# A table of 1,574 entries orders all operations of a fused attention and gated-MLP kernel, in place of its list scheduler

## The chip, the core and the metric

The kernel runs on one core of a Trainium2 chip. The core has four engines that work on data: TensorE (PE in the profile; its weight loads are a row of their own, PEld), VectorE (DVE), ScalarE (ACT) and GpSimd (POOL). SyncE (SP) issues nearly all transfers. Each engine takes its instructions in the order in which the program issues them; an instruction that waits for another engine or for a transfer holds up all that stands behind it on its own engine. The metric is the device time of one execution, in microseconds.

## What is computed

The reference, cut to what matters: capped attention over 4 batches of 12 heads, 448 positions and 64 columns, and behind it a gated MLP with a spatial gate.

```python
scores = scale * np.matmul(q, k.transpose(0, 1, 3, 2))
scores = cap * np.tanh(scores / cap)
attn = np.exp(scores - max); attn = attn / (np.sum(attn, -1) + 1e-09)
x = np.matmul(attn, v)                       # heads side by side: (4, 448, 768)
h = gelu_tanh(x @ w_in)                      # 1024 columns
u, v = h[..., :512], h[..., 512:]
v_n = (v - mean) / np.sqrt(var + 1e-06) * g_ln
v_s = np.einsum('ts,bsd->btd', w_sg, v_n) + b_sg[None, :, None]
out = x + (u * v_s) @ w_out
```

## The kernel before

**Tiling.** The 12 heads of a batch are six pairs; a pair is called batch.pair here, so 0.3 is the fourth pair of batch 0. Two pairs make a group. The 448 key positions of a pair are three blocks of 128 and a tail of 64; the tails of both pairs of a group are worked on together, as block 0 of the first pair. A unit is one block: `scores` (matmuls into one of two PSUM tiles `sc`), tanh and exp on ACT over 128x896 (L635, L637) into one of five tiles `p`, and `values` (L594, L604). There are 84 units. Most scores and the MLP's matmuls run as three products of a high and a low part, so that q and k, the weights and the activations are split first: a cast gives the high part (`cop`, L338 on DVE or L340 on ACT), a subtraction on DVE the low part (`sub`, L368). q and k of a pair lie in one of three tiles `raw`.

**Sums.** The softmax denominators are matmuls with ones (`den_op`, L504). In nine of twelve groups DVE first adds the `p` tiles of a pair (`add`, L647). `recip` copies the sums out, sends them through DRAM (four transfers out, one in), takes reciprocals on DVE (L683, L686) and sends them out again four times; `norm` reads each pair's row back, spread over 128 partitions (L725, tile `n`), and multiplies (L728).

**MLP of a batch (`gated`).** `hv` (L785), `hu` (L825), `vsg` (L842) and `outp` (L863) are the matmul groups; `hv 0.3` is tile 0, chunk 3. Between them lie gelu (L766 and L771 on ACT, L768 and L773 on DVE), layer norm and the gate. They accumulate in PSUM tiles `ps`, of which there are three.

**Weights.** w_in and w_out come as 64-bit words and are decoded: `decode` loads a piece of 512 or 384 KB into one of six stages (L420), four operations on DVE or ACT take the words apart (L426, L432, L436, L441), one on POOL adds them (L446), and a cast and a subtraction split the result.

**What sets the order.** All this is recorded as operations by `op`, each with its engine (or two engines, `BOTH`, for casts and copies), an estimated cost, a key and its buffers. `Plan.run` (L173) is a list scheduler: it steps an estimated clock, takes from the operations that are ready on an engine the one with the least key, chooses the engine of a `BOTH` operation, and issues it. The order in which it issues is the program order of each engine. The keys come from numbers at the top of the file (`ATT`, `GATED`, `FETCH_W` and others).

**Transfers.** `fetch` (L536) loads q and k of a pair in two transfers of 224 KB, from arrays `q2` and `k2`. Only the very first, q of pair 0.0, is issued on ACT's queue; SP issues the rest.

Of the kernel before, what the change touches and what calls it, by code (L numbers as in the profile page):

```python
# [49 lines left out]
DEN = 14.19  # L50
TVAL = 21.27
TPOS = 1
TPOS0 = 3
DEC_AHEAD = 219.05

ISSUE = 0.45
LAT = {
    ("pe", "pe"): 0.0, ("pe", "pool"): 0.08, ("pe", "act"): 0.04, ("pe", "dve"): 0.04, ("pe", "sp"): 0.03,
    ("act", "act"): 0.025, ("act", "dve"): 0.033, ("act", "pe"): 0.052, ("act", "pool"): 0.08, ("act", "sp"): 0.03,
    ("dve", "dve"): 0.031, ("dve", "act"): 0.034, ("dve", "pe"): 0.054, ("dve", "pool"): 0.08, ("dve", "sp"): 0.03,  # L60
    ("pool", "pool"): 0.03, ("pool", "act"): 0.035, ("pool", "dve"): 0.035, ("pool", "pe"): 0.054,
    ("pool", "sp"): 0.03, ("sp", "sp"): 0.03, ("sp", "pe"): 0.06, ("sp", "act"): 0.04, ("sp", "dve"): 0.04,
    ("sp", "pool"): 0.08,
}
OVERLAP = {"act": 0.099, "dve": 0.08, "pool": 0.0, "sp": 0.0, "pe": 0.0}
# [18 lines left out]
class Buf:  # L84
    def __init__(self, pool=None, t=None, cls=None):
        self.pool, self.t, self.cls = pool, t, cls
        self.hist, self.left, self.end = [], 0, 0.0
        self.queued = pool is None
        self.on_free = None
        self.first = None  # L90


class Pool:
    def __init__(self, tiles, caps=None):
        self.free = [(-1.0, i, t) for i, t in enumerate(tiles)]
        self.n = len(tiles)
        self.queues = {}
        self.caps = caps or {}
        self.held = {}

    def add(self, when, t):
        self.free.append((when, self.n, t))
        self.n += 1

    def can(self, bufs):
        by = {}
        for b in bufs:
            k = by.get(b.cls, 0)
            q = self.queues[b.cls]
            if len(q) <= k or q[k] is not b:  # L110
                return None
            by[b.cls] = k + 1
            if self.held.get(b.cls, 0) + k + 1 > self.caps.get(b.cls, 99):
                return None
        if len(self.free) < len(bufs):
            return None
        return sorted(self.free)[len(bufs) - 1][0]

    def take(self, b):
        e = min(self.free)  # L120
        self.free.remove(e)
        self.queues[b.cls].popleft()
        self.held[b.cls] = self.held.get(b.cls, 0) + 1
        b.t = e[2]
# [12 lines left out]
class Plan:
# [3 lines left out]
    def op(self, eng, cost, fn, rd=(), wr=(), key=0.0, mode=None, size=0, fast=False):  # L141
        o = Op()
        o.engs = {eng: (cost, fn)} if isinstance(eng, str) else {e: (cost(e), lambda e=e: fn(e)) for e in eng}
        o.key, o.mode, o.size, o.fast = round(key, 6), mode, size, fast
        o.succ, o.weak, o.npred, o.ready, o.alloc, o.num = [], [], 0, 0.0, [], len(self.ops)
# [27 lines left out]
    def run(self):  # L173
        engines = ("pe", "act", "dve", "pool", "sp")
        free = dict.fromkeys(engines, 0.0)
        cand = {e: [] for e in engines}
        mode, wire, left, last = None, 0.0, len(self.ops), 0.0
        port = {"dve": 0.0, "pool": 0.0}

        def ready(o):  # L180
            for e in o.engs:
                cand[e].append(o)

        for o in self.ops:
            if not o.npred:
                ready(o)
        while left:
            best = None
            for e in engines:
                ests, f = [], free[e]  # L190
                for o in cand[e]:
                    t = o.ready if o.ready > f else f
# [778 lines left out]
```

## Time and profile before

| what | us |
|---|---|
| median of 3 runs | 383.86 (381.99 to 384.19) |
| the profiled execution: span from first to last instruction | 380.5 |
| the same execution, outside its span | not shown; the median lies 3.4 above the span |
| PE busy in the span | 371.8 |
| DVE busy | 297.5 |
| ACT busy | 229.4 |
| POOL busy | 43.2 |

The granted TensorE clock is 1.00 in every slice of the span but the last, after the matmuls. Rows of the trace have the start in us from the span's start, the duration, the engine, the line, the operation and the tiles (output <- inputs). Matmul records overlap, since matmuls are pipelined and their ends are modelled. Where PE works without a pause is therefore read from the distance between starts, not from the busy share.

### The profile page before, as it was taken

The numbers are of one execution on the slowest core, as the hardware profiler recorded it, in microseconds if no ns is written. First come the engines' busy times: TensorE is split into PE (matmuls) and PEld (weight loads), VectorE is DVE, ScalarE is ACT, GpSimd is POOL, SyncE is SP. The second block draws the span as 40 slices with busy tenths as digits, with TensorE's granted clock in tenths as the row PEclk, the third lists the DMA queues.
The fourth block names the chain that finished last, engine by engine and source line by source line (L and its number), as shares of the span: only waits on it lengthen the run. The fifth ranks groups of instructions, "written<-read, shape, count | busy, mean of one in ns | idle before, by whom it ended". The sixth has DMA issues, their size and how long they took to land.

```text
span 380.5 us, 5588 instructions
## 1 busy us (share of the span) xinstructions
PE 371.8 (98%) x2064; PEld 250.7 (66%) x2064; DVE 297.5 (78%) x530; ACT 229.4 (60%) x306; POOL 43.2 (11%) x38
## 2 busy tenths in 40 slices
PE   8989999999999999999999999999999999999996
PEld 4333344343899536745888866445889889889995
DVE  2699999899999999999869688765386796365633
ACT  5978999999655599578633356996134323143210
POOL 0121055010432110132001000000010000010000
PEclk9999999999999999999999999999999999999999
DMA  7984542864342354155222002200222102100003
GB/s 247 342 319 138 188 154 57 260 198 147 112 137 70 94 161 138 46 174 169 90 81 80 18 28 69 68 5 24 70 68 63 35 24 82 41 0 24 2 0 145
DMA packets 26298, 39.65 MB, mean 104 GB/s; under 512 B 5824, under 2 KB 23712, under 8 KB 26272
## 3 DMA queue, kind: packets, MB, share of 16 engines
q1 hardware_dynamic: 25984, 38.96, 32.0%
q8 instruction: 16, 0.26, 0.3%
q10 hardware_dynamic: 288, 0.34, 0.3%
q14 instruction: 10, 0.08, 0.1%
HBM read 33.28 MB, written 6.02 MB: 103 GB/s over the span
## 4 chain that ended last, share of the span: by engine, by line
PE 61%; DVE 19%; DMA 9%; issue 4%; ACT 3%; SPq 2%; POOL 1%; DVEq 0%; ACTq 0%; POOLq 0%
PE ps L863 11%; PE ps L825 10%; PE ps L785 8%; PE ps L594 7%; PE ps L842 7%; PE sc L562 6%; PE sc L863 5%; DMA raw<-in_k_dram 4%; DVE p L647 3%; PE sc L785 2%; DMA stage<-in_w_in_dram 2%; PE sc L825 2%; PE den L504 2%; DVE rg L368 2%; DVE hl L338 1%
## 5 line engine op out<-in xcount | busy, mean ns | idle before, releaser
L635 ACT ACTIVATE p<-sc,qsc 128x896 f32<-128x896 f32 x84 | 81.0, 1010 | 14.0 <-DVE p L647 4.8
L637 ACT ACTIVATE p<-p,first_sb 128x896 f32<-128x896 f32 x84 | 83.7, 1049 | 0.1
L594 PE MATMUL ps<-p,v 128*64 128x448 f32 x288 | 62.5, 552 | 0.1
L647 DVE TENSOR_TENSOR p<-p,p 128x896 f32<-128x896 f32 (+1 forms) x48 | 53.5, 1114 | 9.4 <-ACT p L637 8.6
L562 PEld LDWEIGHTS sc<-hl 64*128 64x128 f32 x378 | 32.5, 184 | 30.3 <-ACT p L635 17.8
L825 PE MATMUL ps<-rg,win 128*128 128x448 f32 x241 | 51.6, 364 | 0.0
L562 PE MATMUL sc<-hl 64*128 64x448 f32 x378 | 50.1, 388 | 1.4 <-ACT p L635 1.4
L446 POOL TENSOR_TENSOR stage<-stage 128x512 int32<-128x512 int32 (+1 forms) x20 | 34.2, 1714 | 128.7 <-DVE stage L441 116.0
L785 PE MATMUL ps<-win,rg 128*128 128x512 f32 x205 | 48.4, 392 | 0.0
L825 PEld LDWEIGHTS ps<-rg,win 128*128 128x128 f32 x241 | 45.0, 187 | 4.0 <-DVE t L773 0.2
L766 ACT ACTIVATE t<-ps 128x448 f32<-128x448 f32 (+1 forms) x26 | 14.7, 565 | 48.7 <-PE ps L785 34.2
L785 PEld LDWEIGHTS ps<-win,rg 128*128 128x128 f32 x205 | 38.5, 188 | 8.3
L863 PE MATMUL ps<-rg,wout 128*128 128x448 f32 x175 | 41.3, 367 | 0.0
L594 PEld LDWEIGHTS ps<-p,v 128*64 128x64 f32 x288 | 17.3, 136 | 35.2 <-issue 20.6
L863 PEld LDWEIGHTS ps<-rg,wout 128*128 128x128 f32 x175 | 32.5, 188 | 4.7 <-issue 2.0
L768 DVE SCALAR_TENSOR_TENSOR t<-t,ps 128x448 f32<-128x448 f32 (+1 forms) x26 | 16.8, 646 | 17.7 <-ACT t L766 17.7
L842 PE MATMUL ps<-wsg,rg 128*128 128x448 f32 x130 | 30.0, 365 | 0.2 <-DVE rg L368 0.2
L771 ACT ACTIVATE t<-t 128x448 f32<-128x448 f32 (+1 forms) x30 | 18.1, 604 | 18.7 <-DVE t L768 18.6
L801 POOL TENSOR_TENSOR sm<-sm,pw 128x1 f32<-128x1 f32 x14 | 8.8, 630 | 170.1 <-DVE sm L798 170.1
L842 PEld LDWEIGHTS ps<-wsg,rg 128*128 128x128 f32 x130 | 24.1, 188 | 3.8 <-issue 1.4
L340 ACT ACTIVATE rg<-u 128x448 fp32r<-128x448 f32 x15 | 8.6, 579 | 28.3 <-DVE u L851 28.3
L863 PE MATMUL sc<-rg,wout 128*128 128x448 f32 x89 | 22.0, 367 | 0.0
(115 smaller groups left out, 455.4 us busy)
## 6 DMA issues: line engine op xcount, KB each, us to landing
stage<-in_w_in_dram SPq DMA_DIRECT2D x12, 512.0 KB
raw<-in_k_dram SPq DMA_DIRECT2D x24, 224.0 KB
n<-spread SPq DMA_DIRECT2D x24, 224.0 KB
raw<-in_q_dram SPq DMA_DIRECT2D x23, 224.0 KB
out_dram<-x SPq DMA_DIRECT2D x23, 224.0 KB
v<-in_vp_dram SPq DMA_DIRECT2D x24, 192.0 KB
stage<-in_w_out_dram SPq DMA_DIRECT2D x8, 384.0 KB
u<-in_w_sgT_dram SPq DMA_DIRECT2D x4, 224.0 KB
```

The costliest lines, as they stand in the source:

```text
L446: nc.gpsimd.tensor_tensor(out=a.bitcast(I32), in0=a.bitcast(I32), in1=hi, op=ALU.add)
L562: nc.tensor.matmul(out=sc.t[:, h, :S], lhsT=hl[s].t[rows, w, 1, 128 * c - 128:128 * c], rhs=hl[s].t[rows, m, 0], start=(k == 0), stop=(k = ...
L594: nc.tensor.matmul(out=pav[s].t[64 * h:64 * h + 64, :S], lhsT=v[s].t[:, 128 * (c - 1) + 64 * h:128 * (c - 1) + 64 * h + 64], rhs=p.t[:, h, ...
L635: op("act", c_act(2 * S, True, True), lambda p=p, sc=sc: nc.scalar.activation(out=p.t, in_=sc.t[:, :, :S], func=ACTF.Tanh, scale=qsc), rd= ...
L637: op("act", c_act(2 * S, False, True), lambda p=p: nc.scalar.activation(out=p.t, in_=p.t, func=ACTF.Exp, scale=cap_sb), rd=[k_first], wr=[ ...
L647: op("dve", c_tt(2 * S), lambda: nc.vector.tensor_tensor(out=a.t[rows], in0=a.t[rows], in1=p.t[rows], op=ALU.add), rd=[p], wr=[a], key=ake ...
L768: op("dve", c_tt(n), lambda: nc.vector.scalar_tensor_tensor(out=view(), in0=view(), scalar=1.0 / GELU_A, in1=src(), op0=ALU.add, op1=ALU.m ...
L771: op("act", c_act(n), lambda: nc.scalar.activation(out=view(), in_=view(), func=ACTF.Tanh, scale=GELU_C * GELU_A), wr=[sq], key=key)
L785: nc.tensor.matmul(out=ps.t[:, :HF], lhsT=(xl if a else xh)[c].t[:, t * 128:t * 128 + 128], rhs=win[w][:, c, HF:], start=(c == 0 and k == ...
L825: nc.tensor.matmul(out=ps.t[:, :S], lhsT=win[w][:, c, f * 128:(f + 1) * 128], rhs=(xl if a else xh)[c].t[:, :S], start=(c == 0 and k == 0) ...
L842: nc.tensor.matmul(out=ps.t[:, :S], lhsT=(vl if a else vh)[c].t[:, f * 128:(f + 1) * 128], rhs=wsg[w][:, c, :], start=(c == 0 and k == 0), ...
L863: nc.tensor.matmul(out=ps.t[:, :S], lhsT=wout[w][:, f, c * 128:(c + 1) * 128], rhs=(gl if a else gh)[f].t[:, :S], start=(f == 0 and k == 0 ...
```

## The change

The scheduler goes. `Plan.run` walks a table, `ORDER`, of 1,574 entries. An entry is twice the number of an operation, plus one where the operation goes to the second of its two engines (`BOTH` is DVE, then ACT). Operations are numbered as the source calls `op`, from 0: `first` is 0, `consts` 1, the memset `zeros` 6, so that the table's first entry, 12, is `zeros`, and 336 is operation 168, the load of q of pair 0.0. Keys and their constants go; estimated costs stay as unused arguments. Free tiles of a pool are handed out first in, first out.

q and k lie in one array, and a pair's are loaded in one transfer of 448 KB, except in the first group, where pairs 0.0 and 0.1 keep two transfers of 224 KB each. Loads of w_sg and of b_sg are recorded after the attention of batch 0 and have no wait of their own any more. The two operations `slack`, which issued no instruction, go. Of the sums' transfers only the order changes.

```diff
     def run(self):
-        engines = ("pe", "act", "dve", "pool", "sp")
-        free = dict.fromkeys(engines, 0.0)
...
-                pick = min(
-                    (x for x in ests if x[0] <= first),
-                    key=lambda x: (x[1].key + (SWITCH if e == "pe" and x[1].mode != mode else 0.0)
-                                   + (SHARED[e] if len(x[1].engs) > 1 else 0.0), x[1].num))
...
+        assert len(ORDER) == len(self.ops)
+        for code in ORDER:
+            o = self.ops[code // 2]
+            assert not o.npred, o.tag
             for b in o.alloc:
                 b.pool.take(b)
...
+            list(o.engs.values())[code % 2][1]()
...
+ORDER = (
+    12, 336, 14, 2, 0, 338, 340, 342, 344, 16, 4, 350, 420, 6, 8, 348, 346, 358, 32, 352, 364, 360, 372, 10, 366, 354,
+    380, 362, 356, 422, 20, 18, 374, 428, 368, 22, 24, 370, 382, 430, 392, 26, 376, 400, 384, 432, 378, 394, 34, 386,
...
             def fetch(s):
-                for n, src in enumerate((q2, k2)):
-                    queue = nc.sync if g or s or n else nc.scalar
-                    op("sp", ISSUE, lambda s=s, n=n, src=src, queue=queue: queue.dma_start(
-                        out=raw[s].t[:, n, :], in_=src[b, pairs[s]]),
-                       wr=[(raw[s], n)], key=base - FETCH_G + s * 3 if g else -99.0 + 0.5 * s, size=128 * S * 4)
+                if g:
+                    load(name("qk", s), lambda: raw[s].t, lambda: qk[b, pairs[s]], [raw[s]], 2 * 128 * S * 4)
+                    return
+                for n in range(2):
+                    load(name("qk", s, n), lambda n=n: raw[s].t[:, n, :], lambda n=n: qk[b, pairs[s], :, n],
+                         [(raw[s], n)], 128 * S * 4, queue=nc.sync if s or n else nc.scalar)
...
-        "q2": byhead(q),
-        "k2": k2,
+        "qk": _np.stack([byhead(q), k2], axis=3),
```

The table read out, in the places that the prediction speaks of. On the left the order in which the scheduler before issued; `in 0.1` is chunk 0, second half, of w_in.

```
SP, from the start, with the KB up to and with each transfer
before  first, 0.0 q (on ACT), 0.0 k, 0.1 q, 0.2 q, 0.2 k, 0.1 k, consts, 0.0 v, 0.0 vt, 0.2 vt, 0.1 v,
        0.2 v, in 0.1 (2664), in 1.1, in 2.1, in 3.1, in 4.1, sg 0, 0.3 q, 0.3 k (5384), 0.4 q, 0.4 k, ...
table   0.0 q (on ACT), consts, first, 0.0 k, 0.1 q, 0.1 k, 0.0 v, in 0.1 (1704), 0.2 qk (2152), 0.0 vt,
        0.1 v, in 1.1, 0.3 qk (3368), 0.2 vt, 0.4 vt, 0.4 qk, in 2.1, 0.2 v, in 3.1, 0.5 qk, in 4.1, ...
SP, batch 0's reciprocals, table
        recip out 3, 2, 1.3 v, recip out 1, 0, 1.5 qk, 1.4 vt, recip in 0, sg 2, sg 3, recip in 1, 1.4 v,
        recip in 2, 1.5 v, in 4.0, recip in 3, recip in 4, ...
ACT     before  0.2 tanh 1, 0.1 exp 3, 0.2 exp 1, 0.2 tanh 0      table   0.2 tanh 1, 0.2 tanh 0, 0.1 exp 3
DVE     table   recip 0, 1.1 add 3, 1.3 lo, 1.4 hi, in 3.0 high and shift, in 4.1 hi, in 2.0 low,
                in 3.0 low, 1.4 lo, in 2.0 sign, 1.1 x, norm 0
DVE     table   in 5.1 lo, x hi 0, 1.2 x, norm 1, in 3.1 lo, norm 2, x lo 0, x hi 1, in 4.0 high, x lo 1
PE      before  1.5 score 1 and 2, 1.4 value 0, 2, 3, 1.5 score 3, ..., 2.0 score 2, 2.0 score 3, 2.1 score 1, hv 0.0
        table   1.5 score 1 and 2, 1.4 value 0, 2, 3, hv 0.0, 1.0, 0.1, 1.1, 1.5 score 3, 2.0 score 1, ...
casts and copies: 56 go from ACT to DVE, 18 from DVE to ACT; transfers of q and k: 48 before, 26 in the table
```

## Rows read from the trace of the kernel before

**Rows 1.** The page's first part: busy us, share of the span, instructions.

```profile
PE 371.8 (98%) x2064; PEld 250.7 (66%) x2064; DVE 297.5 (78%) x530; ACT 229.4 (60%) x306; POOL 43.2 (11%) x38
```

**Rows 2.** Windows: length, then busy us of PE, PEld, DVE, ACT, POOL; clock; DMA share, GB/s.

```profile
0.00:13.80 13.80, 12.04 (x62) 5.72 (x66) 3.89 (x11) 9.69 (x12) 0.20 (x4) 1.00 0.80 252
10.00:20.00 10.00, 10.00 (x76) 3.71 (x72) 6.88 (x11) 10.00 (x12) 2.72 (x2) 1.00 0.97 347
13.80:47.80 34.00, 31.51 (x206) 11.04 (x198) 33.88 (x57) 29.47 (x34) 5.42 (x4) 1.00 0.70 245
47.80:94.40 46.60, 46.60 (x318) 18.25 (x318) 45.40 (x72) 46.20 (x52) 11.59 (x6) 1.00 0.53 160
94.40:188.40 94.00, 93.40 (x527) 64.23 (x526) 89.86 (x172) 68.64 (x96) 20.11 (x14) 1.00 0.41 123
188.40:269.50 81.10, 81.10 (x450) 55.90 (x449) 57.42 (x90) 45.25 (x59) 1.96 (x3) 1.00 0.15 47
269.50:376.90 107.40, 107.12 (x513) 95.53 (x511) 66.45 (x132) 30.20 (x57) 3.89 (x7) 1.00 0.13 44
```

**Rows 3.** Timeline of PE, 19 to 41 us: start, length, line, tiles, records, wait.

```profile
19.42 0.96 PE L570 MATMUL sc<-raw 64*64 64x448 f32 x3
21.35 0.97 PE L570 MATMUL sc<-raw 64*64 64x448 f32 x4 [0.97 <-DMA raw<-in_k_dram]
22.25 0.88 PE L562 MATMUL sc<-hl 64*128 64x448 f32 x6
...
32.25 1.72 PE L594 MATMUL ps<-p,v 128*64 128x448 f32 x8
33.90 0.98 PE L570 MATMUL sc<-raw 64*64 64x448 f32 x8
34.81 0.88 PE L562 MATMUL sc<-hl 64*128 64x448 f32 x6
35.62 1.72 PE L594 MATMUL ps<-p,v 128*64 128x448 f32 x8
38.74 0.88 PE L562 MATMUL sc<-hl 64*128 64x448 f32 x6 [1.40 <-ACT p L635]
```

**Rows 4.** Timeline of ACT, 19 to 41 us, the three instructions that waited.

```profile
22.36 1.90 ACT L635 ACTIVATE p<-sc,qsc 128x896 f32<-128x896 f32 x2 [2.03 <-PE sc L570]
...
37.68 1.01 ACT L635 ACTIVATE p<-sc,qsc 128x896 f32<-128x896 f32 x1 [1.84 <-DVE p L647]
39.36 1.01 ACT L635 ACTIVATE p<-sc,qsc 128x896 f32<-128x896 f32 x1 [0.67 <-DVE p L647]
```

**Rows 5.** Timeline of SP, the first two issues and the load of `in 4.0`.

```profile
0.74 0.40 SPq L355 DMA_DIRECT2D first_sb<-in_first_dram  x1
1.20 0.43 SPq L536 DMA_DIRECT2D raw<-in_k_dram  x1
...
90.65 0.38 SPq L420 DMA_DIRECT2D stage<-in_w_in_dram  x1
```

**Rows 6.** Timeline of DVE: the the first weight piece, and five other instructions.

```profile
13.80 0.43 DVE L432 TENSOR_SCALAR stage<-stage 128x512 f32<-128x512 f32 x1 [3.00 <-DMA stage<-in_w_in_dram]
...
15.63 1.54 DVE L432 TENSOR_SCALAR stage<-stage 128x512 f32<-128x512 f32 x1
...
61.69 0.67 DVE L686 RECIPROCAL d<-d 64x84 f32<-64x84 f32 x1
...
71.94 0.63 DVE L728 TENSOR_TENSOR x<-x,n 128x448 f32<-128x448 f32 x1 [1.09 <-DMA n<-spread]
...
94.96 0.41 DVE L432 TENSOR_SCALAR stage<-stage 128x512 f32<-128x512 f32 x1
...
178.39 1.32 DVE L368 TENSOR_TENSOR rg<-x,rg 128x448 fp32r<-128x448 f32 x1
```

**Rows 7.** Timeline of POOL, 14 to 24 us, the first decode.

```profile
15.59 1.30 POOL L446 TENSOR_TENSOR stage<-stage 128x512 int32<-128x512 int32 x1 [15.15 <-DVE stage L441]
```

**Rows 8.** Timeline of PE around 140 us.

```profile
138.81 0.97 PE L594 MATMUL ps<-p,v 128*64 128x448 f32 x4
140.38 0.96 PE L504 MATMUL den<-p,const_sb 128*32 128x448 f32 x8 [0.60 <-DVE p L647]
```

**Rows 9.** Groups by line: mean ns stands behind the busy us; casts and adds.

```profile
L647 DVE TENSOR_TENSOR p<-p,p 128x896 f32<-128x896 f32 (+1 forms) x48 | 53.5, 1114 | 9.4 <-ACT p L637 8.6 <-PE ps L594 0.2
...
L441 DVE SCALAR_TENSOR_TENSOR stage<-stage 128x512 int32<-128x512 int32 (+1 forms) x20 | 12.6, 632 | 0.2
...
L340 ACT ACTIVATE rg<-x 128x448 fp32r<-128x448 f32 x13 | 6.4, 563 | 0.0
L338 DVE COPY x<-ps 128x448 f32<-128x448 f32 x20 | 12.2, 614 | 1.0 <-PE ps L594 0.9
L338 DVE CAST rg<-x 128x448 fp32r<-128x448 f32 x10 | 3.8, 381 | 0.0
```

**Rows 10.** Waits of ACT between 47.8 and 94.4: total, times, longest us.

```profile
ACT p L635 <- PE den L504: 0.4, 1, 0.4
```

More of the change, by code (lines that the diff above doesn't have):

```diff
@@ L94, in __init__ @@
     def __init__(self, tiles, caps=None):
-        self.free = [(-1.0, i, t) for i, t in enumerate(tiles)]
+        self.free = deque(tiles)
         self.n = len(tiles)
@@ L98, in __init__ @@
         self.caps = caps or {}
[L99 to L117, printed above, removed]
-    def take(self, b):
[L120 to L124, printed above, removed]
+    def take(self, b):
+        assert self.queues[b.cls].popleft() is b
+        b.t = self.free.popleft()
     def give(self, b):
-        self.held[b.cls] -= 1
         if b.on_free is None or not b.on_free(b):
-            self.add(b.end, b.t)
+            self.free.append(b.t)
 class Op:
-    __slots__ = ("engs", "cost", "fn", "key", "mode", "bufs", "alloc", "succ", "weak", "npred", "ready", "size",
-                 "num", "fast")
+    __slots__ = ("tag", "engs", "mode", "bufs", "alloc", "succ", "weak", "npred", "size", "num", "fast")
 class Plan:
@@ L464, in freed @@
         for k in range(3):
-            r_p.add(b.end, t[:, k, :])
+            r_p.free.append(t[:, k, :])
         return True
     def weights():
-        for h, keys in ((1, IN_V), (0, IN_U)):
+        for h in (1, 0):
             for c in range(KD):
-                decode(("in", c, h), win, w_in, c, slice(HF * h, HF * h + HF), keys[0] + keys[1] * c)
-        for c in range(NC):
-            split_sg(c)
+                decode(("in", c, h), win, w_in, c, slice(HF * h, HF * h + HF))
         n = DM // 2
@@ L509, in den_op, with den_unit @@
             done[0] += len(units)
-            op("pe", mms(4, sets=1, records=4 * len(units)), fn, rd=[k_const] + [u[2] for u in units], wr=[den], key=key, mode="D")
-        def den_unit(p, kind, src, key, last=False):
+            op("%d sum %d" % (b, n0), "pe", whole4(), fn, rd=[k_const] + [u[2] for u in units], wr=[den], mode="D")
+        def den_unit(p, kind, src, last=False):
             waiting.append((p, kind, src))
             if len(waiting) == 2 or last:
-                den_op(waiting[:], key)
+                den_op(waiting[:])
                 waiting.clear()
@@ L903 @@
         if not b:
-            bias([xs[0, NP - 1]])
+            load("bias", lambda: bsg_sb, lambda: b_sg.partition_broadcast(128), [k_bsg], 230000)
+            for c in range(NC):
+                split_sg(c)
         if b:
```

443 lines of the change are left out of this document (158 added, 285 removed), and 77 rows, old and new, of the table ORDER.

## The prediction

> **What bounds the kernel now.** I read the page's first part, then the windows, then the timelines of PE and ACT where the windows showed a gap, and last what had let the late instruction go. PE is busy for 371.8 of 380.5 us [rows 1]. That share can't be taken as the room that is left, since records of matmuls overlap; so I go by the windows and the starts. From 188.4 us on PE is without a hole (81.10 of 81.10, then 107.12 of 107.40), while DVE rests for 64.6 of these 188.5 us [rows 2]: there the order of other engines' work can change nothing as long as it is not late. Between 47.8 and 94.4 PE, DVE (45.40 of 46.60) and ACT (46.20) are full together [rows 2]. The holes lie in front of that: between 13.8 and 47.8 PE is busy for 31.51 of 34.00, ACT for 29.47, and DVE is full (33.88) [rows 2]. So an order can win what these holes hold, and little else; the matmuls are the same in number and shape.
>
> Two holes carry the sum. The first: a group's tail scores (L570) begin at 19.42 and the next piece at 22.25, 2.83 us later; the same piece without a wait takes 0.91 (33.90 to 34.81). That is 1.92 us, and what came last was k of a pair [rows 3]. ACT stood for 2.03 in front of the tanh of that block [rows 4]. The second: eight records of `values` begin at 35.62 and the next piece at 38.74, 3.12 us later, against 1.65 for eight such records before (32.25 to 33.90), so 1.47 us, waiting for ACT [rows 3]. ACT in turn waited 1.84 and then 0.67 us for two adds on DVE (L647), which release a tile `p` [rows 4]. DVE was not resting: it was late because decode work stood in front of the adds. A third and smaller hole: at 140.38 a sum waits 0.60 us for an add; start to start it is 1.57 against 0.83 for half of the eight records above, 0.74 lost [rows 3, 8].
>
> **The change, part by part.**
>
> *The start.* The table lets SP issue `consts` ahead of `first`. Issues on SP stand 0.46 us apart [rows 5], and the first scores and the scale of the tanh need `first`; k of 0.0 behind it is late by as much. Bounds: nothing, if q on ACT's queue came last anyway, and 0.46 plus a little for the 39 KB. I take +0.46.
>
> *Transfers in the first 25 us.* They move 252 GB/s up to 13.8 us and 347 from 10 to 20 [rows 2], so that a transfer's place in the queue sets its time. k of 0.3, which the tail scores of pairs 0.2 and 0.3 wait for, had 5,384 KB up to and with it; in the table it has 3,368. That is 2,016 KB less, 2.06 MB, and at 347 GB/s 5.9 us earlier: about 16.4 instead of 22.3. Its tile is free once the tail scores of 0.0 are done, long before. ACT would take that tanh in the slot in which it began to wait, 22.36 - 2.03 = 20.33 [rows 4], and the scores need 0.91, so k has three us to spare. The hole goes: bounds -1.92 (PE) and -2.03 (ACT). What is moved back pays: 0.2's q and k have 2,152 KB in place of 1,184, 0.99 MB at 252 GB/s, 3.9 us later. Their scores come near 17 us, two units before the wait, and they land near 11 by the same rate, so this costs nothing; if the split on DVE, which now stands behind the four decode operations of one weight piece (0.43 to 0.63 each [rows 6, 9]), were late, it would cost up to 1.
>
> *One transfer for q and k.* 48 issues become 26. At 0.46 us [rows 5] that is 10 us of SP's time over the span, hidden, as SP mostly waits. The bytes are the same. Queued transfers of 224 KB already ran at 347 GB/s with the DMA engines at 0.97 [rows 2], so I take nothing for the size; bounds 0 and, if the rate rose by a tenth, 2 us of landing time that nothing waits for once the hole is closed.
> The Trainium skill (DMA: Bandwidth & Descriptors, Bandwidth) wants transfers of at least 1 MiB and gives 138 GB/s for 64 KB and 341 for 1 MB, each alone; by it the merging itself would be a gain, and the 347 GB/s of this trace say otherwise for transfers in a queue. The sum is the same by either, since no term of it has the merging's rate.
>
> *Decode work against adds on DVE.* The first weight piece landed at 13.80, DVE having waited 3.00 for it [rows 6], with 2,664 KB up to and with it; in the table it is 1,704. 0.98 MB at 252 GB/s: DVE starts to decode 3.9 us earlier. Besides, eight instructions that stood ahead of the first of the two late adds (four of decode's L441 at 0.63 [rows 9], three others of decode at some 0.4 [rows 6] and a copy of 0.61 [rows 9]) stand behind it, about 4 us, and two of about 0.5 stand in front instead: 3 us earlier still. The add ended 1.84 us too late for ACT. So both waits go, 1.84 + 0.67 on ACT, 1.47 plus some remainder on PE. Up to 94.4 us ACT and PE are both full, hence what is won arrives whole only where both win: PE's 1.92 + 1.47 = 3.39 is the lower bound, ACT's 2.03 + 1.84 + 0.67 = 4.54 the upper one. I take 4.3, nearer to ACT's, since ACT is the fuller of the two in the stretch behind the holes but one (46.20 of 46.60, with every PE piece there started by a tanh or an exp).
>
> *Casts from ACT to DVE.* 56 go to DVE, 18 copies to ACT. A cast of 128x448 is 0.38 on DVE and 0.56 on ACT [rows 9]. Counted along the table, DVE has 11 of them more and 14 copies and casts less ahead of batch 0's gate, 2.9 against 4.9 us: 2 us less in the stretch in which DVE is full. The rest, some 11 us more, falls where DVE rests for 64.6 us [rows 2]. Nothing for either; if DVE had no rest there, 11 us.
>
> *MLP matmuls set among attention.* PE changes its kind of work 131 times in place of 139, and the changes that follow `values` or an MLP piece, which cost about 0.1, are 47 in both. Nothing; bounds -0.5 and +0.5. Four pieces of `hv` now come before 1.5's last score. The second needs the PSUM tile that 1.4's copy on ACT releases, and stands one piece, 0.69 us, behind the last matmul of that pair, less than the copy and two hand-overs take: +0.3. The other tiles of `ps` come free at least 1.2 us of PE work ahead, where one add to the residual is due, and at least 3.0 where the four steps of a gelu are. The sum at 140 us has its add further ahead in the table: -0.7.
>
> **The sum.** +0.46 - 4.3 - 0.7 + 0.3 = -4.2 us, on a span of 380.5: 376.3. Around the span I change nothing; the last matmuls and the store are the same. The median of the runs is 383.86, 3.36 above this execution's span, so I forecast 383.86 - 4.2 = 379.6, which I put at 379.5. One per cent, about what a measurement of this kernel can tell from no change, is 3.84 us: the bound is 380.0.
>
> **The rivals.**
>
> *Half of it comes back through waits on DVE.* Between the start of a reciprocal and the first `norm` lie two trips through DRAM, 61.69 to 71.94, 10.25 us, and DVE already waited 1.09 at the end [rows 6]. In the table only eleven instructions, 6.2 us, and the reciprocal's 0.67 stand between: DVE would stand up to 3.4 us where it is full. Further, SP holds `in 4.0` back until a stage is free (`in 5.1 lo`), and DVE comes to `in 4.0 high` eight instructions and 3.3 us later, while the load issued at 90.65 was decoded from 94.96 on [rows 5, 6], 4.3 later: another 1. For it: in-order DVE, full at that place. Against: the 3.9 us of lead from the earlier start, which the 4.4 eat up, and the scores and adds behind. If PE sees half of 4.4, it is -4.2 + 2.2 = -2.0: 381.9.
>
> *Slower: DVE and POOL collide.* A cast or scalar operation on DVE takes 1.54 in place of 0.43 when POOL's decode runs beside it (15.63 against 15.59 to 16.89) [rows 6, 7]. Sixteen instructions of the trace are long in this way, the last at 178.39 (1.32 in place of about 0.6) [rows 6]. If the moved casts and the new order make all twenty decodes and the fourteen powers hit one each, that is 18 more, 1.1 each, 20 us of DVE; 64.6 us of rest take what falls behind 188 us, but the share in front, where 31 of POOL's 43 us lie [rows 2], is 10 to 13. It decides once it exceeds DVE's lead of 3.9 and the gain of 4.2: at 11, 383.86 - 4.2 + 7.1 = 386.8. Against it: DVE has fewer of these casts, not more, up to 140 us. The Trainium skill (GPSIMD Engine Reference, the table of specifications) says that GpSimd's SBUF interfaces are shared with VectorE and that DVE instructions of two ports or two SBUF inputs contend; by that rule this rival has its mechanism, and the trace's 1.54 agrees.
>
> *The change does nothing.* PE is full at 98%, and a hole that closes opens again a unit later, because PE, ACT and DVE are full together behind it: 383.9. For it speaks 47.8 to 94.4; against it, that ACT's waits there sum to 0.4 us [rows 10] and ACT would simply start that stretch earlier.
>
> **How the numbers follow.** The forecast has 0.62, its own range 376.3 (4.54 and 0.74 won, the +0.46 and +0.3 not paid, and 2.3 for smaller holes that I left out) to 381.0 (3.39 won, and 0.5 each for casts and changes of kind); seven eighths of it lie below 380.0. The first rival 0.24, the slower one 0.07, nothing 0.07. Faster by over 1%: 0.62 x 7/8 = 0.54. Slower by over 1%: 0.07. Within: 0.39. The range reaches from 376.3 to 383.3: it leaves out the slower rival, about half of nothing and a little below.
>
> **What would show each step.** Start: first scores near 4.3 instead of 3.9. Transfers: no wait for k at 20 us, the first decode on DVE near 10. Adds: no wait of ACT for L647 before 48 us, and the stretch up to batch 0's first `hv` shorter by 4 us. Casts: DVE busy about 9 us more in all, 2 less before 140. The first rival shows as DVE waiting for `n<-spread` or for a weight load between 60 and 80 us; the slower one as more long DVE instructions beside POOL. The forecast is wrong if PE's starts after 94 us show waits of over 1 us, since I looked there at PSUM tiles alone, not at every chain across engines.

## The result, and the profile after

| | before | changed |
|---|---|---|
| median of six runs each, us | 382.28 (380.35 to 384.19) | 378.22 (377.56 to 379.16) |
| profiled span, us | 380.5 | 376.9 |
| end of the last matmul, us | 376.83 | 372.97 |

The ratio is 0.9896, with a 95% interval of 0.9867 to 0.9925: 4 us or 1.0% faster, against 379.5 forecast (376.3 to 383.3). Three more runs of before had brought its median down from 383.86 to 382.28. The experiments have runs of before of their own, with medians of 381.80, 382.20 and 381.93; each ratio below is taken against these, and a difference of less than half a microsecond between medians that were not measured together means little.

The page's first part and, up to 269.5 us, the windows of the changed kernel, to be laid beside [rows 1, 2]:

```profile
PE 371.1 (98%) x2064; PEld 251.2 (67%) x2064; DVE 300.4 (80%) x568; ACT 212.5 (56%) x268; POOL 37.2 (10%) x38
```

```profile
0.00:13.80 13.80, 12.10 (x46) 4.91 (x48) 7.30 (x17) 8.37 (x10) 1.77 (x5) 1.00 0.77 253
10.00:20.00 10.00, 10.00 (x76) 3.67 (x72) 6.58 (x11) 9.63 (x11) 2.88 (x2) 1.00 0.49 150
13.80:47.80 34.00, 34.00 (x238) 13.07 (x236) 28.26 (x49) 32.94 (x37) 3.92 (x3) 1.00 0.64 217
47.80:94.40 46.60, 46.43 (x309) 19.96 (x306) 42.80 (x71) 43.61 (x52) 8.81 (x6) 1.00 0.60 180
94.40:188.40 94.00, 94.00 (x545) 61.62 (x543) 88.94 (x176) 68.78 (x90) 16.29 (x14) 1.00 0.42 120
188.40:269.50 81.10, 81.10 (x440) 58.78 (x439) 62.43 (x108) 37.99 (x47) 2.19 (x3) 1.00 0.15 46
```

Between 13.8 and 47.8 us PE has no hole left (34.00 of 34.00, 31.51 before). DVE, full there before (33.88), now rests for 5.7 us, and in 47.8 to 94.4 for 3.8 (1.2 before). The transfers between 10 and 20 us run at 150 GB/s, not at 347: something held them back.

To compare kernels of different order I use a lag. Each kind of matmul piece gets the distance to the next start that a quarter of such pieces keep below (before and changed kernel together). The lag at a time is that time less the sum of these distances over the pieces started so far. It rises where PE waits. Here are all profiles, with each kernel's median (4 to 18 runs each):

| kernel | 13.8 us | 24 | 48 | 100 | 370 | median us |
|---|---|---|---|---|---|---|
| before | 2.8 | 4.9 | 7.8 | 9.2 | 14.4 | 381.8 to 382.3 |
| changed | 4.7 | 4.9 | 5.5 | 6.8 | 10.5 | 378.2 |
| e1_first_ahead | 2.6 | 2.7 | 3.3 | 4.6 | 8.4 | 377.5 |
| e2_old_order | 3.5 | 3.7 | 5.4 | 7.9 | 12.9 | 381.4 |
| e3_new_then_old | 4.0 | 4.2 | 4.8 | 13.9 | 19.2 | 387.4 |
| e4_old_then_new | 2.9 | 4.7 | 6.2 | 7.7 | 11.5 | 379.1 |
| e5_warm | 3.5 | 3.7 | 4.3 | 5.9 | 9.6 | 377.4 |
| e6_two_transfers | 4.2 | 4.4 | 5.0 | 6.3 | 10.1 | 378.1 |
| e7_old_engines | 3.0 | 3.1 | 3.7 | 7.5 | 14.4 | 383.2 |
| e8_norm_later | 3.4 | 3.6 | 4.1 | 5.4 | 9.2 | 378.3 |
| e9_one_copy | 3.4 | 3.6 | 4.2 | 7.1 | 10.8 | 379.3 |
| e10_late_engines | 4.2 | 4.4 | 5.0 | 6.3 | 12.6 | 379.7 |
| e11_k_second | 3.4 | 3.6 | 4.2 | 5.5 | 9.2 | 377.3 |
| e12_decode_ahead | 3.0 | 3.1 | 5.3 | 6.8 | 10.6 | 379.9 |

Read the first two rows: the changed kernel is 1.9 us behind at 13.8 us, level at 24, 2.3 ahead at 48, 2.4 at 100 and 3.9 at the end.

### The profile page after: what moved, and what is told of

Same layout as the page of the kernel before. It is cut to its first block, busy times and chain, and to the rows that moved or that the text cites. A ratio compares the mean times of both kernels' runs of the same rounds, so it can differ in the third digit from the quotient of the medians.

```text
span 376.9 us, 5496 instructions
## 1 busy us (share of the span) xinstructions
PE 371.1 (98%) x2064; PEld 251.2 (67%) x2064; DVE 300.4 (80%) x568; ACT 212.5 (56%) x268; POOL 37.2 (10%) x38
## 4 chain that ended last, share of the span: by engine, by line
PE 96%; DMA 1%; DVE 1%; issue 0%; ACT 0%; SPq 0%; DVEq 0%; ACTq 0%
PE ps L538 15%; PE ps L748 13%; PE ps L710 12%; PE sc L506 12%; PE ps L785 11%; PE ps L765 7%; PE den L448 5%; PE sc L785 5%; PE sc L710 3%; PE sc L514 3%; PE sc L748 3%; PE ps L548 3%; PE sc L765 2%; PE sc L522 2%; DMA raw<-in_qk_dram 1%; DVE stage L379 0%
## 5 line engine op out<-in xcount | busy, mean ns | idle before, releaser
L748 PEld LDWEIGHTS ps<-rg,win 128*128 128x128 f32 x224 | 41.7, 188 | 6.2 <-issue 2.2
L785 PE MATMUL ps<-rg,wout 128*128 128x448 f32 x188 | 44.4, 366 | 0.0
L710 PEld LDWEIGHTS ps<-win,rg 128*128 128x128 f32 x187 | 35.0, 188 | 7.7 <-issue 0.7
L393 POOL TENSOR_TENSOR stage<-stage 128x512 int32<-128x512 int32 (+1 forms) x20 | 25.7, 1290 | 137.1 <-DVE stage L388 67.2
L785 PEld LDWEIGHTS ps<-rg,wout 128*128 128x128 f32 x188 | 34.9, 188 | 4.8 <-issue 1.7
L724 POOL TENSOR_TENSOR sm<-sm,pw 128x1 f32<-128x1 f32 x14 | 11.3, 818 | 170.0 <-DVE sm L722 170.0
L765 PE MATMUL ps<-wsg,rg 128*128 128x448 f32 x112 | 25.9, 366 | 0.0
L765 PEld LDWEIGHTS ps<-wsg,rg 128*128 128x128 f32 x112 | 20.7, 188 | 3.2 <-issue 1.0
L323 DVE TENSOR_TENSOR hl<-raw,hl 128x832 fp32r<-128x832 f32 x21 | 22.4, 1065 | 0.2
L448 PE MATMUL den<-p,const_sb 128*32 128x448 f32 x160 | 19.7, 550 | 0.0
```

The costliest lines, as they stand in the source:

```text
L323: op(tag, "dve", c_tt(n), lambda: nc.vector.tensor_tensor(out=out(), in0=a(), in1=b(), op=ALU.subtract), rd=rd, wr=wr, fast=True)
L393: nc.gpsimd.tensor_tensor(out=a.bitcast(I32), in0=a.bitcast(I32), in1=hi, op=ALU.add)
L448: nc.tensor.matmul(out=den.t[32 * j:32 * j + 32, :S], lhsT=ones_sb[:, kind, NP - 1 - kind - p:NP + 31 - kind - p], rhs=src.t[:, h, :], sta ...
L710: nc.tensor.matmul(out=ps.t[:, :HF], lhsT=(xl if a else xh)[c].t[:, t * 128:t * 128 + 128], rhs=win[w][:, c, HF:], start=(c == 0 and k == ...
L748: nc.tensor.matmul(out=ps.t[:, :S], lhsT=win[w][:, c, f * 128:(f + 1) * 128], rhs=(xl if a else xh)[c].t[:, :S], start=(c == 0 and k == 0) ...
L765: nc.tensor.matmul(out=ps.t[:, :S], lhsT=(vl if a else vh)[c].t[:, f * 128:(f + 1) * 128], rhs=wsg[w][:, c, :], start=(c == 0 and k == 0), ...
```

## The experiments

**The start.** PE of before and of the changed kernel, and DVE and SP of the changed kernel in the first 25 us:

```profile
3.86 1.70 PE L578 MATMUL sc<-raw,first_sb 64*128 64x448 f32 x4 [0.28 <-DMA first_sb<-in_first_dram]
5.38 0.93 PE L578 MATMUL sc<-raw 64*128 64x448 f32 x4
```

```profile
3.95 1.86 PE L522 MATMUL sc<-raw,first_sb 64*128 64x448 f32 x4 [0.37 <-DMA first_sb<-in_first_dram]
6.01 3.36 PE L522 MATMUL sc<-raw 64*128 64x448 f32 x8 [0.20 <-DMA raw<-in_qk_dram]
```

```profile
9.01 0.43 DVE L379 TENSOR_SCALAR stage<-stage 128x512 f32<-128x512 f32 x1
...
22.17 0.59 DVE L295 CAST hl<-raw 128x832 fp32r<-128x832 f32 x1 [4.82 <-DMA raw<-in_qk_dram]
```

```profile
10.95 0.33 SPq L315 DMA_DIRECT2D raw<-in_qk_dram  x1
11.32 5.78 SPq L315 DMA_DIRECT2D vt<-in_vt_dram  x2
17.20 0.38 SPq L315 DMA_DIRECT2D raw<-in_qk_dram  x1
```

k of 0.0 is late, as it stands third on SP. But the eight records behind it took 3.36 us; the first four of the eight in before took 0.93. Experiment 1 gives SP the old first two issues:

```diff
-ORDER = (12, 336, 14, 2, 0, 338, ...
+ORDER = (12, 336, 14, 0, 2, 338, ...
```

> The changed kernel with one exchange in the table: SP issues first ahead of consts, as before. Theory (the lag at the start, 1.97 us at 13.8 us by the starts of PE, comes from k of pair 0.0, which landed at 6.0 in place of 5.4 us, and from the plain matmuls, which then ran at 0.95 us a record up to 10.1 us in place of 0.54 from 5.4 us on): the short records return before 6 us and the kernel gains most of these 2 us, 376.0 to 376.8 us against 378.2. Rival (the lag is made by the other changes of order, or is swallowed by waits that come later, as the first two holes of before swallowed theirs): 377.9 to 378.5.

377.52 us (four runs, 376.52 to 378.48), ratio 0.9888 [0.985, 0.9925]. In its profile the gain is the whole two us (lag 2.6 at 13.8), and every later column keeps it:

```profile
5.39 2.06 PE L522 MATMUL sc<-raw 64*128 64x448 f32 x8
```

The median has only 0.7 of it and lies between the two theories. The runs lie in two pairs, 1.7 us apart, so that something at the start differs from run to run of one kernel. How long the plain score records are in a profile, and when that ended, seemed to follow from the pause of PE in front of the first score. Experiment 5 takes the pause away:

```diff
-WCOLS = 208
+WCOLS = 256
```

> The changed kernel with its three warm-up matmuls made 256 columns wide instead of 208, so that they end near 4.1 us and PE does not stand (0.24 to 0.38 us in the profiles so far) before the first score. Nothing else. Theory (where that pause is 0.24 or 0.28 us the first records of the scores are 0.54 us long from about 5 us on, where it is 0.37 or 0.38 us they stay at 0.95 us until 7.7 to 10.3 us; it is the pause, not the data, that makes the changed kernel's start slow): the first score begins 0.2 us later, the records are short by 6 us, the starts of PE at 13.8 us lag by 1 to 2 us less, and the time is 376.2 to 377.4 instead of 378.2, with less scatter. Rival (the start waits for k alone): no gain, 378.2 to 378.6.

377.42 us, ratio 0.9882 [0.9865, 0.99]: at the edge of the range, but not by this mechanism, and the interval overlaps that of the changed kernel. The pause is gone and the records nevertheless stayed at 0.95 us until past 7 us. In experiment 8, where PE waited 0.48 us before the first score and k came at 6.22, they were short from the second score on. The length of the records, in the changed kernel and in experiment 8 (duration in ns, minimum, median, maximum):

```profile
L522 PE MATMUL sc<-raw x8: 951/951/1110, 6.0 to 8.4; 64*128 64x448 f32 x8
```

```profile
L522 PE MATMUL sc<-raw x8: 536/536/640, 6.2 to 7.5; 64*128 64x448 f32 x8
```

So my theory of the pause fell. The granted clock reads 1.00 (the higher level, 2.4 GHz) in every slice of 1 us between 4 and 11 us of the changed kernel, and doesn't tell the two apart. From one pair of records that run side by side to the next it is 0.75 us in the long state (6.92, 7.66, 8.41 in the changed kernel) and 0.37 in the short one (6.70, 7.07, 7.45 in experiment 8). That is a factor of two, the same that a granted clock of 0.50 makes in experiment 3 below; that the clock was low here too without the rows showing it is a rival that no run tests. In 14 profiles the records became short somewhere between 4.8 and 10.3 us; what sets it stays open. What the order sets is when k lands. Experiment 11 puts it second:

```diff
-SP: consts, first, 0.0 k, 0.1 q, ...
+SP: first, 0.0 k, consts, 0.1 q, ...
```

> The changed kernel with SP's first three issues as first, k of 0.0, consts (in the table they are consts, first, k). Theory (k of 0.0 landing late is worth 0.6 us: the second score begins at 5.1 to 5.6 us in the four profiles with first ahead, at 5.7 to 6.2 in the six with consts ahead; whatever the start gains is kept to the end): second score at 5.0 to 5.4 us, 377.4, 376.8 to 377.9. Rival (the moment at which the records get short decides the start, and that does not follow from the landing): the second score is earlier and the median stays at 378.2.

377.30 us (376.62 to 377.39), ratio 0.9866 [0.9839, 0.9892]. All six runs lie below all six of the changed kernel, 0.9 us by the medians, though the two intervals of the ratios overlap. Its median is the lowest here, but those of experiments 1 and 5 lie within 0.3. The second score starts at 5.57, later than the theory had it; over the five profiles with `first` ahead it starts at 5.41 on average (5.10 to 5.61), over the nine with `consts` ahead at 5.94 (5.67 to 6.23). In this profile the records were long until past 7 us, in the changed kernel's until past 10, so that the gain can't be divided between the landing of k and the records.

**The early part against the late part.** Experiment 2 keeps the whole old order as a table, with the old engines of all casts; only the merging is new.

```diff
-ORDER = <the new table>
+ORDER = <the old order, qk where q was>
```

> The changed kernel's source with the whole old order as its table, q and k of a pair at the place where q was issued. Only the scheduler is gone and the transfers are merged. Theory (the gain is the order's): the two waits of PE at 22 and 38 us stay, and the time is that of before within 0.7 us, 381.6 to 383.0. Rival (merging the transfers is worth something of its own, by earlier landing): k of pair 0.3 comes earlier, the wait at 22 us shrinks by 1 us or more, 380 to 381.3.

381.44 us (ten runs), ratio 0.9991 [0.9976, 1.0007]: the same as before, as the first theory had it. But the two waits did not stay. The first weight piece is decoded from 11.80 (13.80 before), PE does not wait at 20 to 22, and at 36 it is 1.79 us from eight records of `values` to the next piece, where before had 3.12 [rows 3]:

```profile
11.80 0.44 DVE L379 TENSOR_SCALAR stage<-stage 128x512 f32<-128x512 f32 x1 [0.68 <-DMA stage<-in_w_in_dram]
```

```profile
20.17 0.98 PE L514 MATMUL sc<-raw 64*64 64x448 f32 x8
21.08 0.87 PE L506 MATMUL sc<-hl 64*128 64x448 f32 x6
...
34.44 1.72 PE L538 MATMUL ps<-p,v 128*64 128x448 f32 x8
36.23 0.87 PE L506 MATMUL sc<-hl 64*128 64x448 f32 x6
...
83.20 0.95 PE L448 MATMUL den<-p,const_sb 128*32 128x448 f32 x4
84.39 0.94 PE L448 MATMUL den<-p,const_sb 128*32 128x448 f32 x4 [0.25 <-DVE p L589]
85.27 0.97 PE L538 MATMUL ps<-p,v 128*64 128x448 f32 x4
```

The 2.4 us that it leads at 48 us shrink at once where a sum waits for an add (83.20 to 85.27 is 2.07 for eight records, against 0.89 for eight, 37.03 to 37.92, undisturbed in this profile) and are 1.3 at 100. That the transfers landed 2 us earlier is not the merging's doing. Experiment 4, below, has the same first 21 transfers of SP, merged likewise (k of 0.3 is in the 19th), and up to 25 us the same work in the same order on the other engines, and there the first piece is decoded from 13.54 and PE waits for k again, 1.64 us by the distance of starts:

```profile
13.54 0.43 DVE L379 TENSOR_SCALAR stage<-stage 128x512 f32<-128x512 f32 x1 [2.63 <-DMA stage<-in_w_in_dram]
```

```profile
21.17 0.97 PE L514 MATMUL sc<-raw 64*64 64x448 f32 x4 [0.68 <-DMA raw<-in_qk_dram]
```

So landings differ by 1.7 us between executions of one beginning, and the wait for k comes or stays away with them: with the old beginning two profiles of three have it (13.8 to 24 us in the table of lags), with the new one none of eleven.

Experiments 3 and 4 join the two orders at the first score of 1.0.

```diff
-ORDER = <the new table>
+ORDER = <its first 185 entries> + <what is left, in the old order>
```

> The table's first 185 entries (up to the first score of pair 1.0, 45 us) and then all that is left in the old order. Theory by the starts of PE: up to 48 us the change is worth 2.4 us, behind it 1.5 us. So 382.3 - 2.4 = 379.9, 379.2 to 380.6. Rival (what is won early is taken back as soon as PE, ACT and DVE are full together): 381.5 to 382.5.

387.39 us, ratio 1.0147 [1.0116, 1.0177]: 5.6 us slower than before, and outside both theories. What is left has the old engines too. One place has the loss:

```profile
54.51 1.71 PE L448 MATMUL den<-p,const_sb 128*32 128x448 f32 x4 [5.04 <-DVE p L589]
56.14 1.76 PE L538 MATMUL ps<-p,v 128*64 128x448 f32 x4
57.84 1.54 PE L548 MATMUL ps<-p,vt 64*64 64x448 f32 x8
59.31 0.86 PE L506 MATMUL sc<-hl 64*128 64x448 f32 x6
```

```profile
46.35 0.42 DVE L295 CAST win<-stage 128x512 fp32r<-128x512 f32 x1
46.81 0.69 DVE L323 TENSOR_TENSOR win<-stage,win 128x512 fp32r<-128x512 f32 x1
...
49.26 0.68 DVE L388 SCALAR_TENSOR_TENSOR stage<-stage 128x512 int32<-128x512 int32 x1
49.86 1.08 DVE L589 TENSOR_TENSOR p<-p,p 128x896 f32<-128x896 f32 x1
50.86 1.51 DVE L379 TENSOR_SCALAR stage<-stage 128x512 f32<-128x512 f32 x1
52.29 2.16 DVE L589 TENSOR_TENSOR p<-p,p 128x896 f32<-128x896 f32 x1
```

The new early part has put weight work off. The old order, taken from there, does that work first, and the adds of 0.5 stand behind it; two instructions beside POOL's decode are long as well (1.51 for 0.43, 2.16 for 1.08).

The wait of 5.04 us is not all of it. PE stood from 49.47. The granted clock fell to 0.50 (the lower level, 1.2 GHz) at 52.19, while PE stood, and was back at 1.00 at 59.02, when PE had worked for 4.5 us:

```profile
49.47:52.19 2.72, 0.00 (x0) 0.00 (x0) 2.72 (x3) 1.82 (x2) 2.17 (x2) 1.00 0.61 168
54.51:59.02 4.51, 4.51 (x16) 0.79 (x16) 4.51 (x8) 2.87 (x3) 0.00 (x0) 0.50 0.04 11
```

From 54.51 to 59.31 PE started four records of the sums, four of `values` and eight of the tails. At a clock of 1.00 this profile has 0.89, 1.65 and 0.92 us for eight of each, so 2.2 us in place of 4.8: some 2.6 us of the loss are the clock. Nothing of the loss comes back.

```diff
-ORDER = <the new table>
+ORDER = <the same 185 operations, in the old order> + <the rest of the new table>
```

> The same 185 operations in the old order and then the rest of the table. Theory: the early 2.4 us are not won, the late 1.5 us are: 382.3 - 1.5 = 380.8, 380.2 to 381.5. Rival (the late part rests on the lead that DVE gets early: the wait of 2.9 us for the first norm then reaches PE): 382 or more.

379.14 us, ratio 0.9924 [0.99, 0.9948]: 2.7 us faster, 1.2 more than the theory had. By the distance of starts the wait for k at 22 us is there again (1.64, though q and k are merged), but at 37 only 0.29 of the 1.47 is left. Two instructions of weight work (1.1 us) that stand ahead of the second add of 0.3 in before stand behind it here, and the add starts 1.7 us earlier (36.47, before 38.18). Putting work off is not the only thing that closes this wait: experiment 2 puts nothing off, and its wait is gone; it began to decode 2 us earlier. And in before the first add of 0.3 is itself long, 1.86 us for 1.07, beside a decode on POOL:

```profile
35.34 1.29 POOL L446 TENSOR_TENSOR stage<-stage 128x512 int32<-128x512 int32 x1 [12.68 <-DVE stage L441]
```

```profile
35.72 1.86 DVE L647 TENSOR_TENSOR p<-p,p 128x896 f32<-128x896 f32 x1
```

That is 0.8 of the 1.84 us for which ACT waited. It does not make the wait of PE alone, as this add is as long in experiments 2 and 4 (1.87 and 1.90). In the changed kernel both adds of 0.3 take 1.07 (at 33.88 and 35.56), and POOL's next decode starts at 38.25. Experiment 12 tests the putting off in the table itself: five decode instructions, 2.5 us, in front of the adds of 0.3.

```diff
-DVE: 0.3 add 2, in 0.0 high, in 0.0 low, 0.3 add 3, in 0.0 shift, in 4.1 sign, in 0.0 sign
+DVE: in 4.1 sign, in 0.0 high, in 0.0 low, in 0.0 shift, in 0.0 sign, 0.3 add 2, 0.3 add 3
```

> The changed kernel with five decode instructions on DVE (2.5 us: four steps of in 0.0 and the last of in 4.1) put ahead of the two adds of pair 0.3 at 34 to 36 us. Theory (the adds release the tiles p for ACT, which has no room there: the tanh of 0.4 waited 0.16 us for one already; what ACT loses is not won back): ACT waits 1.7 to 2.4 us for L589 again, as before the change, and the time is 1.5 to 2.2 us longer, 379.7 to 380.4. Rival (DVE has 2.9 us of rest at the first norm, so the loss is made up there): within 0.5 us of 378.2.

379.91 us (378.31 to 381.49), ratio 0.9951 [0.9925, 0.9978]. The lag rises by 2.2 between 24 and 48 us instead of 0.6, and stays. ACT waits as before the change, 1.89 in two pieces:

```profile
34.62 1.01 ACT L576 ACTIVATE p<-sc,qsc 128x896 f32<-128x896 f32 x1 [0.80 <-DVE p L589]
36.73 1.01 ACT L576 ACTIVATE p<-sc,qsc 128x896 f32<-128x896 f32 x1 [1.09 <-DVE p L589]
```

Again a part of it is an add made long, by 0.9 us, beside a decode on POOL (33.61 to 35.69) that the moved instructions set off earlier:

```profile
34.63 2.00 DVE L589 TENSOR_TENSOR p<-p,p 128x896 f32<-128x896 f32 x1
```

The rest of DVE at the first norm gave nothing of this back.

**The merging.** Experiment 6 takes it out of the changed kernel:

```diff
-load(name("qk", s), lambda: raw[s].t, lambda: qk[b, pairs[s]], [raw[s]], ...)
+for n in range(2):
+    nc.sync.dma_start(out=raw[s].t[:, n, :], in_=qk[b, pairs[s], :, n])
```

> The changed kernel with q and k of a pair as two transfers of 224 KB, one right after the other, everywhere. 22 issues more on SP. Theory (the bytes set the landing, and SP mostly waits): the same within 0.4 us, 377.8 to 378.6. Rival (the merging is what closes the wait for k of 0.3, since in the old order with merged transfers that wait was gone): a wait for k at 20 us comes back, 379 or more.

378.08 us, ratio 0.9893 [0.9876, 0.9909]: the same, with no wait for k. The lag table has the same steps as for the changed kernel, to 0.1 us, after the start.

**The engines of the casts.** Experiment 7 gives all 74 moved casts and copies their old engine, in the new order:

```diff
-ORDER = <the new table>
+ORDER = <the same operations in the same order, 74 codes changed by one>
```

> The changed kernel's order with the 74 casts and copies on the engines that the scheduler gave them (56 back to ACT, 18 back to DVE). Theory (the choice of engine is worth nothing, as DVE and ACT both rest where most of them lie): 377.7 to 378.9. Rival (in the stretch in which ACT and DVE are both full the order only works with its own choice: ACT or DVE comes late for the adds and the tanh): 380 or more.

383.20 us (twelve runs), ratio 1.003 [1.0011, 1.0048]: all that the change had won is gone, and my theory with it. By the distance of starts, its waits of PE lie at 83 (1.69), 97 (1.09), 103 (0.47) and 173 us (0.67 and 0.59). Experiment 9 changes a single one:

```diff
-849    (operation 424, the copy 1.4 x, on ACT)
+848    (on DVE)
```

> The changed kernel with one copy on the other engine: 1.4 x (the copy of pair 1.4's result out of PSUM) on DVE, as before, instead of on ACT. Theory (with the 74 old engines PE waited 1.69 us at 83 us for just this copy, before the second piece of hv, and every piece of lag that arises after 48 us stays to the end): 378.2 + 1.7 = 379.9, 379.2 to 380.5. Rival (the wait needs the whole lot of moved casts, DVE being late from them, not from this copy's place): within 0.4 us of 378.2.

379.32 us, ratio 0.9928 [0.99, 0.9956]; 1.1 us by the medians, and in the profile 1.6 (from 48 to 100 us the lag grows by 2.9, in the changed kernel by 1.3):

```profile
82.08 0.40 PE L710 MATMUL ps<-win,rg 128*128 128x512 f32 x1
83.88 0.74 PE L710 MATMUL ps<-win,r 128*128 128x512 f32 x2 [1.39 <-DVE x L295]
```

```profile
82.20 1.08 DVE L589 TENSOR_TENSOR p<-p,p 128x896 f32<-128x896 f32 x1
83.20 0.62 DVE L295 COPY x<-ps 128x448 f32<-128x448 f32 x1
```

The copy takes 0.62 us on DVE and 0.55 on ACT; what costs is that on DVE it stands behind an add, while `hv 1.0` waits for the PSUM tile that it reads. On ACT it runs as soon as PE has finished the pair, and the same step of PE is 0.23 instead of 1.80:

```profile
83.01 0.55 ACT L297 ACTIVATE x<-ps 128x448 f32<-128x448 f32 x1 [0.73 <-PE ps L538]
```

Experiment 10 takes the 64 that run after 100 us:

```diff
-ORDER = <the new table>
+ORDER = <the same, 64 codes behind 100 us changed by one>
```

> The changed kernel with the old engine for the 64 moved casts and copies that run after 100 us; the ten before it as in the table. Theory (of the 5 us that the 74 cost, 1.7 is the copy 1.4 x and some 1.7 more at 97 to 103 us come from DVE's casts just ahead, so that the rest falls behind 170 us): 378.2 + 2.0 = 380.2, 379.6 to 381. Rival (behind 100 us ACT and DVE both have rest, as the prediction had it, and the late waits only follow from the early ones): within 0.5 us of 378.2.

379.71 us, ratio 0.9938 [0.9912, 0.9964]. Behind 100 us the lag grows by 6.3 instead of 3.7. The largest piece, at 169 to 174 us:

```profile
170.94 0.52 ACT L297 ACTIVATE wout<-stage 128x384 fp32r<-128x384 f32 x1
171.35 1.04 ACT L578 ACTIVATE p<-p,first_sb 128x896 f32<-128x896 f32 x1
173.25 1.01 ACT L576 ACTIVATE p<-sc,qsc 128x896 f32<-128x896 f32 x1 [0.86 <-DVE p L589]
```

```profile
171.49 0.56 DVE L323 TENSOR_TENSOR wout<-stage,wout 128x384 fp32r<-128x384 f32 x1 [2.17 <-ACT wout L297]
172.12 1.09 DVE L589 TENSOR_TENSOR p<-p,p 64x896 f32<-64x896 f32 x1
```

A cast of 0.52 us queues on ACT behind an exp and a copy; DVE stands 2.17 us for it with its subtraction, an add stands behind that, and ACT waits for the add.

**The wait at the first norm.** DVE of the changed kernel did stand where the first rival said:

```profile
71.88 0.63 DVE L656 TENSOR_TENSOR x<-x,n 128x448 f32<-128x448 f32 x1 [2.90 <-DMA n<-spread]
```

Experiment 8 fills the wait with work that stood behind it:

```diff
-DVE: 1.1 x, 0 norm 0, in 5.1 hi, 1.5 qk hi, in 3.0 sign, 1.5 qk lo
+DVE: 1.1 x, in 5.1 hi, 1.5 qk hi, in 3.0 sign, 1.5 qk lo, 0 norm 0
```

> The changed kernel with four DVE instructions (2.7 us: casts and subtractions of in 5.1 and pair 1.5, a step of in 3.0) put ahead of batch 0's first norm, in which DVE waited 2.90 us for the transfer. Theory (that wait costs nothing, because PE and ACT are full there and DVE catches up): the wait is gone from DVE and the time is the same within 0.3 us, 377.9 to 378.5. Rival (PE sees half of the wait, as the prediction's first rival has it): 1.4 us faster, 376.8.

378.31 us, ratio 0.9897 [0.9879, 0.9915]: the same. The 2.90 us cost nothing.

## Why the prediction was right

The steps against the lag of the profiles (the changed kernel's less before's, in us of PE):

| step | forecast | read from the lag |
|---|---|---|
| start | +0.46 | +2.0 (to 13.8 us) |
| the two waits at 22 and 38 us | -4.3 | -4.3 (13.8 to 48: -1.9 and -2.4) |
| 48 to 100, with `hv` ahead of the last score (+0.1 of it read) | +0.3 | 0 |
| 100 to 130 | 0 | +0.4 |
| the sum at 140 | -0.7 | -0.7 |
| 250 to 310 | 0 | -1.0 |
| what is left, 150 to 250 and the end | 0 | -0.2 |
| all | -4.2 | -3.9 at the last matmul, -3.6 in the span |

Part of the agreement is luck: in these two profiles the start costs 1.5 us more than forecast, and a stretch for which nothing was forecast gives 1.0 back. The time itself lies 1.3 under the forecast as before's median of three runs was 1.6 too high; from 382.28 the same sum gives 378.1.

**The start** is the term that was mis-sized. That `first` would be late was the wrong half: the first score starts at 3.95 (3.86 before), and what counts is k, half a us late. I had priced both at one issue of SP. In the profile it became 2.0, because the plain matmuls ran slowly until 10.3 us, which the order was not shown to cause. That is the largest of the nine profiles with `consts` ahead: their lag at 13.8 us is 3.0 to 4.7, on average 3.7, against 3.0 for the five with `first` ahead. So the step costs 0.7 on average; by the medians of experiment 11 it is 0.9. The new order also passes on whatever the start loses or gains: experiments 1, 5, 6, 8 and 11 differ from it at 13.8 us by 0.5 to 2.1 and at 370 by 0.4 to 2.1. Before, two us better at the start, had lost them at 24 us by its wait for k.

**Transfers.** The wait for k of 0.3 is gone, as forecast (19.83 to 20.74 to 21.63, each piece without a wait), in this and in all other profiles with the new beginning. The way there was not the forecast one. "Its tile is free long before" was wrong: SP stood for that tile until 10.95 and then, with the two transfers `vt` behind it, for PE until 17.1. The bytes up to k could not run at 347 GB/s when their issues waited; the window has 150. It sufficed, and DVE's 4.82 us of waiting for 0.4 reached PE in no wait. The first weight piece came at 9.01, ahead of the forecast 10. The prediction also read its window wrongly: what ran at 347 GB/s between 10 and 20 us of before was for the most part not transfers of 224 KB but the five weight pieces of 512 KB that SP issued from 7.10 on (by the order of issue some 2.3 of 3.5 MB, an estimate).

**One transfer for q and k** is worth nothing in the new order (experiment 6), as forecast: 224 and 448 KB give 378.08 and 378.22. The Trainium skill (DMA: Bandwidth & Descriptors, Bandwidth) wants transfers of 1 MiB or more, by rates of transfers that GpSimd issued; no run here has one of q and k, and from 224 to 448 KB no gain shows. In the old order the merging gave no time either (experiment 2).

**Decode against adds** was right in size, and its mechanism is one of two. Of ACT's two waits for L647 [rows 4] a single one of 0.16 is left ahead of 48 us, and experiment 12 brings 1.89 back with 2.5 us of decode. But the prediction left out here that DVE's instructions are long beside POOL's decode: between 13.8 and 47.8 us four are in before (15.63, 18.72, 21.44 and 35.72, 4.1 us too long together), one in the changed kernel (26.01, 0.8). Of the 5.6 us by which DVE's busy time falls there, 33.88 to 28.26, some 3.3 are these and not decode moved behind adds; no run separates what each gave PE. "ACT is the fuller" chose the right end of the bounds. That this gain is kept only with a late part that fits it (experiment 3) I had not seen.

**Casts: "nothing".** The term was right only because the table's choice goes with its order. The reason given, rest of DVE behind 188 us, was no reason: experiments 7, 9 and 10 show that a cast's price is who stands ahead of it and who waits behind it. One copy of 0.6 us is worth 1.1 (medians) to 1.6 (profile), and 64 behind 100 us 1.5 (medians) to 2.6 (lag). DVE's busy time grew by 2.9 us, not by 9, as long instructions became fewer (below). Up to the same piece of PE (`values` of 1.5, 86.61 before and 87.45 after) DVE had 84.6 us of work, by the lengths of its instructions, and now has 80.4; I had counted 2 us less.

**The rivals.** "Half of it comes back" had the place and the size of DVE's wait (2.90, up to 3.4 forecast) and was wrong about who sees it: nobody. "Slower" had its mechanism, but with the sign reversed. It was also priced too low: [rows 2] put 37.3 of POOL's 43.2 us ahead of 188 us, not 31, so that up to 17 of the 20 us would fall there. That a hole which closes opens again shows in experiment 2, whose early lead of 2.4 us was half lost at 100. In the forecast's own range the upper end adds up to 381.5, not 381.0 (383.86 - 3.39 + 0.5 + 0.5 with the start, `hv` and the sum at 140 as forecast).

**Not explained:** the -1.0 between 250 and 310. 0.38 of it is one wait at 307.6 us of before, which is gone. PE changes its kind of work eight times less; I had costed that at nothing, and no run separates it.

## What to carry to other kernels

Price a moved instruction by its queue, not by its length: what stands ahead of it on the new engine, and who waits for it. An order is one thing with its engine choices and with what it puts off; half of a good one, joined to half of another, can be slower than either, so test a part by undoing it in the whole. Look for holes in front of the stretch in which all engines are full: there 2.5 us of DVE work ahead of two adds cost 1.7 us at the end, with an add made long by it, while 2.9 us of DVE waiting 30 us later cost nothing. And before a wait for a transfer is put down to an order, look whether a second profile with the same beginning has it.

## What the hardware showed unexpectedly

The same plain matmul record takes 0.95 or 0.54 us in the first 10 us of a run, at a granted clock of 1.00 in the rows, and the change comes between 4.8 and 10.3 us, with no rule found here.

A wait of PE can cost more than its length: after the 5.04 us of experiment 3 PE worked at a granted clock of 0.50 for 4.5 us, which cost 2.6 more. And transfers issued in the same order landed 1.7 us apart in two profiles (first decode at 11.80 and 13.54, experiments 2 and 4).

DVE instructions over 0.4 us longer than the median of their shape: 14 before (11.3 us together), six in the changed kernel (5.3), the first at 11.25:

```profile
11.25 2.00 DVE L323 TENSOR_TENSOR hl<-raw,hl 128x832 fp32r<-128x832 f32 x1
...
26.01 1.22 DVE L373 TENSOR_SCALAR stage<-stage 128x512 int32<-128x512 uint32 x1
```

POOL's busy time falls with them, 43.2 to 37.2 us for the same 38 instructions, which fits a gain for both engines where they do not meet. The rule of the Trainium skill (GPSIMD Engine Reference, the table of specifications) that the two share SBUF interfaces agrees with that; no run here measured the contention alone.
